# Output projection and attention of token pairs: from a scheduler's order to one written order for five queues

## The chip, the cores and the metric

The kernel runs on one core of a Trainium2 chip. A core has five instruction queues that run beside each other and wait for one another through semaphores: TensorE (PE in the profile, PEld is its weight load), VectorE (DVE, called Vector below), ScalarE (ACT), GpSimd (POOL) and SyncE (SP). TensorE writes to PSUM, of which this kernel uses eight banks of 128 x 512 floats; Vector and ACT read PSUM, POOL works on SBUF alone. SP issues nearly all transfers between HBM and SBUF in this kernel. The metric is the device time of one execution in microseconds.

## What is computed

Tokens S = 2048, width D = 1024, 32 heads of 32. A layer norm feeds two branches, and the output joins them:

```python
xn = _layernorm(x, axis=-1)
s = _A_ref(xn, A_wqkv, A_w_phi, A_wo)
g = _silu(_B_ref(xn, B_w_gate, B_w_up, B_w_down))
return x + s * g
```

`_B_ref` is a gated linear unit with F = 3584. `_A_ref` is linear attention: queries and keys go through a small matrix per head and a double softmax, and then

```python
kv = jnp.einsum("bhsf,bhsd->bhfd", phi_k, v)
z  = jnp.einsum("bhsf->bhf", phi_k)
num = jnp.einsum("bhqf,bhfd->bhqd", phi_q, kv)
den = jnp.einsum("bhqf,bhf->bhq", phi_q, z)[..., None] + 1e-6
o = num / den
return (lambda x, *d: x.transpose(*d))(o, 0, 2, 1, 3).reshape(B, S, D) @ wo
```

The change concerns the end of it: `num` for the queries, the product with `wo`, and `x + s * g`.

## The kernel before, in words

All matrix products are done in float32r with operands cut in two: hi is the value rounded to float32r by ACT (`split`, L129), lo is the rest, subtracted by Vector (L130), and a product is hi·hi + hi·lo + lo·hi (`mm3`, three matmuls, L134 to L136). The large products are block products of 2 x 2 blocks with seven multiplications instead of eight. The seven are named B11, T2, T3, B21, T1, T4 and B22; B11, T2, T3 and T1 open a PSUM bank, and B21, T4 and B22 go on adding into the bank of B11, T3 and T1. So the evacuation of T3 must be read out before T4 starts, that of B11 before B21, that of T1 before B22.

The program runs in stages: projections of Q, K and V, the gated unit, and its down projection (`dsteps`), beside which the attention's features, `kv` and `z` are made. At the end of the down projection the 16 token tiles of 128 have their query features, already divided by the denominator, in `e_d` (HBM), and the gate in `g_d` (HBM). The last stage then goes over eight pairs of token tiles (`NTP` = 8, a pair is 256 tokens). For a pair it does:

- transposes: the features of tile u (0 or 1) and head half hb (0 or 1) are loaded into slot 47 + u (`e_load`) and transposed in two groups q of four 128 x 128 blocks (`phi_transpose`, L662) into two PSUM banks that alternate. ACT copies the hi part and Vector subtracts the lo part into the buffer of (hb, q), of which there are two (`phu`).
- numerators: for each (hb, q), two banks b of four matmuls 128 x 256 each (`numerator`, L680), with two PSUM banks that alternate. ACT copies one half of a bank's rows (L684) and Vector adds the other (L685), into the raw operand `oraw[hb]`.
- operands of the seven products (`o_operands`): B11 needs head half 0 alone; the others need both. POOL makes four differences (L697 to L705), and each operand is cut in hi and lo (L129, L130).
- the seven products with `wo` (held in SBUF), each 4 x 3 matmuls 128 x 512, in banks 103 to 106.
- evacuation: u1 and u2 are built up from B11, T2, T3 (L1217 to L1221); the results of B21, T1, T4 and B22 (L1228, L1231) are multiplied with the gate (L1232) and added to x (L1233), most of it on POOL, and stored. `gx_load` fetches the gate and x rows of the result after next into a ring of two.

The loop of L1203 and on writes, while the products of pair p are issued, the attention of pair p + 1 (`attend`), as whole functions spread over the 28 steps. The instructions are then put in order on each engine by the scheduler of the tile framework, which moves them among each other where their dependences allow it. In the first stage of the program an order written by hand (`FIRST`) is taken word for word instead, with a chain of ordering dependences per engine (`in_order`, L909). The attention of pair 0 runs during the last 14 steps of the down projection.

A turn, in the parts below, is the time from the first B11 product of one pair to that of the next.

Of the kernel before, what the change touches and what calls it, by code (L numbers as in the profile page):

```python
# [49 lines left out]
def hedgehog_glu_kernel(  # L50
# [606 lines left out]
    def phi_transpose(tp_, u, hb, q):  # L657
        ps = tpr.next()
        e = whole(47 + u)
        for j in range(4):  # L660
# [1 line left out]
            nc.tensor.transpose(ps[:, j * P:(j + 1) * P], e[:, k * P:(k + 1) * P], ident)  # L662
# [8 lines left out]
    def numerator(tp_, hb, q):
# [3 lines left out]
        for b in range(2):  # L675
            ps = nmr.next()
            for j in range(2):
                k = 2 * j + b
                for a in range(2):
                    nc.tensor.matmul(ps[:, j * 256:(j + 1) * 256], kg[:, k], ph[:, a, k], start=a == 0, stop=a == 1)  # L680
            hi, lo = [slice(r * 64, r * 64 + 64) for r in (b, 1 - b)]
            o = oraw[hb][hi].rearrange("p u (g t) -> p g u t", t=P)[:, 2 * q:2 * q + 2]
            y, z = [ps[r].rearrange("p (j u t) -> p j u t", j=2, u=2) for r in (hi, lo)]
            nc.scalar.copy(o, z)  # L684
            nc.vector.tensor_add(o, o, y)  # L685
        if q:
            o_operands(tp_, hb)

    def o_operand(tp_, i, b):
        split(pair(of[tp_][i]), b)  # L690

    def o_operands(tp_, hb):
        (b11, b12), (b21, b22) = [(o[:, 0], o[:, 1]) for o in oraw]
        if hb == 0:
            of[tp_] = {i: ofr.next() for i in range(7)}
            o_operand(tp_, B11, b11)
            nc.gpsimd.tensor_sub(b11, b12, b11)  # L697
# [2 lines left out]
        nc.gpsimd.tensor_sub(b12, b22, b12)  # L700
        nc.gpsimd.tensor_sub(b22, b22, b11)
# [488 lines left out]
    def gx_load():  # L1190
        if result:
            tp_, i = result.pop(0)
            t, cols = rows(tp_, i)
            g, xt = gxs[tp_, i] = gx.next(), gx.next()
# [70 lines left out]
```

## Time and profile before

| | us |
|---|---|
| median of 3 runs (2404.22 to 2412.6) | 2407.93 |
| the profiled execution | 2407.68 |
| its span, first to last instruction | 2405.9 |
| start of the last two transpose groups ahead of the last stage | 2175.25 |
| the same to the end of the span | 230.65 |

The page gives the busy time of each engine as a share of the span. The span of an engine's rows that follow each other without waiting says nothing on whether the engine is used at its best, since matmuls are pipelined; from one start to the next is the better measure. A wait is put down to the engine whose signal came last. The profiled execution is slightly longer than its span because the time holds the launch and the end as well.

### The profile page before, as it was taken

How to read it: one execution, taken by the hardware profiler on the slowest of the kernel's cores; microseconds unless marked ns; L12 is line 12 of the kernel's file. 1: busy time of each engine (PE TensorE's matmuls, PEld its weight loads, DVE VectorE, ACT ScalarE, POOL GpSimd, SP SyncE). 2: the span in 40 equal slices, each digit the busy share in tenths (PEclk: the TensorE clock that was granted, in tenths of full speed). 3: DMA queues.
4: the chain of work that ended last, by engine and by line, in shares of the span. 5: the costliest groups of instructions: out<-in, count | busy, mean ns of one | idle time of the engine just before them, and what ended most of it. 6: DMA issues, size and time to landing. Idle time of an engine off the chain costs nothing.

```text
span 2405.9 us, 31955 instructions
## 1 busy us (share of the span) xinstructions
PE 2375.6 (99%) x11008; PEld 1974.5 (82%) x11008; DVE 1759.0 (73%) x2323; ACT 1028.1 (43%) x1536; POOL 957.4 (40%) x611
## 2 busy tenths in 40 slices
PE   9999999999999999999999999999999999999998
PEld 8888888888888878888888888888888888888776
DVE  8636777767676588748867888646888998876776
ACT  7334345444544344324434444423443334454443
POOL 1332456656565422222444232323333435314554
PEclk9999999999999999999999999999999999999999
DMA  7788977777776777786777666586666666877554
GB/s 255 243 303 307 357 273 257 270 260 271 247 276 242 254 278 251 247 280 228 271 262 261 220 219 223 197 274 236 225 222 238 221 221 220 287 257 254 185 184 135
DMA packets 232292, 596.31 MB, mean 248 GB/s; under 512 B 30528, under 2 KB 30528, under 8 KB 227520
## 3 DMA queue, kind: packets, MB, share of 16 engines
q1 hardware_dynamic: 232128, 594.25, 71.8%
q8 instruction: 87, 1.43, 0.2%
q14 instruction: 77, 0.63, 0.1%
HBM read 359.01 MB, written 235.14 MB: 247 GB/s over the span
## 4 chain that ended last, share of the span: by engine, by line
PE 81%; DVE 7%; DMA 5%; issue 3%; ACT 2%; POOL 1%; SPq 0%; ACTq 0%; DVEq 0%; POOLq 0%
PE bank L134 26%; PE bank L135 25%; PE bank L136 25%; DVE w L130 2%; PE bank L283 1%; PE bank L484 1%; DMA fc<-wo 1%; DMA wo_d<-p 1%; DMA fc<-xo_d 1%; PE bank L680 1%; PE bank L662 1%; DMA fc<-qkv_d 1%; DVE p L130 1%; PE bank L903 1%; DVE x L130 0%
## 5 line engine op out<-in xcount | busy, mean ns | idle before, releaser
L134 PE MATMUL bank<-x,w 128*128 128x512 f32 x2352 | 911.6, 390 | 4.4 <-ACT fb L1039 2.5
L135 PE MATMUL bank<-x,w 128*128 128x512 f32 x2352 | 915.6, 389 | 0.0
L136 PE MATMUL bank<-x,w 128*128 128x512 f32 x2352 | 907.4, 389 | 0.0
L129 ACT CAST w<-fa 128x512 fp32r<-128x512 f32 (+1 forms) x430 | 293.6, 686 | 541.8 <-PE bank L135 367.8
L134 PEld LDWEIGHTS bank<-x,w 128*128 128x128 f32 x2352 | 441.6, 188 | 98.3 <-ACT fb L1039 3.5
L136 PEld LDWEIGHTS bank<-x,w 128*128 128x128 f32 x2352 | 441.6, 188 | 91.8 <-DVE w L130 0.4
L135 PEld LDWEIGHTS bank<-x,w 128*128 128x128 f32 x2352 | 441.6, 188 | 90.1
L130 DVE TENSOR_TENSOR w<-fa,w 128x512 fp32r<-128x512 f32 (+1 forms) x430 | 413.1, 965 | 98.5 <-ACT w L129 94.7
L134 PE MATMUL bank<-w,x 128*128 128x512 f32 x708 | 278.9, 394 | 2.6 <-DVE fc L414 2.0
L136 PE MATMUL bank<-w,x 128*128 128x512 f32 x708 | 277.1, 392 | 2.4 <-DVE x L829 2.4
L135 PE MATMUL bank<-w,x 128*128 128x512 f32 x708 | 277.1, 391 | 0.0
L1049 POOL TENSOR_TENSOR fb<-fb,fc 128x512 f32<-128x512 f32 x57 | 88.0, 1544 | 243.7 <-DVE fc L1048 241.0
L136 PEld LDWEIGHTS bank<-w,x 128*128 128x128 f32 x708 | 133.4, 188 | 31.7 <-DVE x L829 2.9
L134 PEld LDWEIGHTS bank<-w,x 128*128 128x128 f32 x708 | 133.3, 188 | 30.5 <-ACT w L129 2.2
L135 PEld LDWEIGHTS bank<-w,x 128*128 128x128 f32 x708 | 133.4, 188 | 26.7 <-DVE w L839 0.2
L619 POOL TENSOR_TENSOR fc<-fc 128x1024 f32<-128x1024 f32 x32 | 81.4, 2542 | 182.9 <-ACT fc L449 126.9
L1048 DVE TENSOR_TENSOR fc<-fc,bank 128x512 f32<-128x512 f32 x84 | 57.3, 682 | 106.8 <-PE bank L136 98.4
L130 DVE TENSOR_TENSOR x<-fa,x 128x512 fp32r<-128x512 f32 x112 | 116.9, 1044 | 24.1 <-ACT x L129 24.1
L129 ACT CAST w<-fb 128x512 fp32r<-128x512 f32 x112 | 69.3, 619 | 128.0 <-PE bank L135 98.2
L130 DVE TENSOR_TENSOR p<-fc,p 128x1024 fp32r<-128x1024 f32 (+2 forms) x97 | 106.6, 1107 | 18.0 <-ACT p L129 15.9
L129 ACT CAST p<-fc 128x1024 fp32r<-128x1024 f32 (+2 forms) x97 | 70.8, 735 | 112.4 <-DVE fc L465 62.7
L130 DVE TENSOR_TENSOR w<-fb,w 128x512 fp32r<-128x512 f32 x112 | 94.2, 842 | 30.1 <-ACT w L129 25.0
(256 smaller groups left out, 3204.8 us busy)
## 6 DMA issues: line engine op xcount, KB each, us to landing
ws_d<-w SPq DMA_DIRECT2D x112, 512.0 KB, 4.2
w<-ws_d SPq DMA_DIRECT2D x112, 512.0 KB, 5.0
fa<-w_gu SPq DMA_DIRECT2D x84, 512.0 KB, 4.0
fa<-h_d SPq DMA_DIRECT2D x84, 512.0 KB, 4.1
fa<-wf_d SPq DMA_DIRECT2D x32, 1024.0 KB, 7.2
h_d<-fc SPq DMA_DIRECT2D x120, 256.0 KB, 3.4
fc<-e_d SPq DMA_DIRECT2D x48, 512.0 KB, 3.8
fc<-qkv_d SPq DMA_DIRECT2D x80, 256.0 KB, 4.3
```

Source lines behind the costliest of these rows:

```text
L129: nc.scalar.copy(o[0], src)
L130: return nc.vector.tensor_sub(o[1], src, o[0].bitcast(F32))
L134: nc.tensor.matmul(o, a[0], b[0], start=first, stop=False, **kw)
L135: nc.tensor.matmul(o, a[0], b[1], start=False, stop=False, **kw)
L136: nc.tensor.matmul(o, a[1], b[0], start=False, stop=last, **kw)
L283: nc.tensor.matmul(ps[:, gs], r[:, gs], bd[:, 4 * f + g], start=True, stop=True)
L484: nc.tensor.matmul(kvb[g // 2][:, g % 2 * 256:g % 2 * 256 + 256], v[:, g].rearrange("p a f -> p (a f)"), ph[:, g].rearrange("p a f -> p (a ...
L619: nc.gpsimd.tensor_mul(ez, e, zb)
L662: nc.tensor.transpose(ps[:, j * P:(j + 1) * P], e[:, k * P:(k + 1) * P], ident)
L680: nc.tensor.matmul(ps[:, j * 256:(j + 1) * 256], kg[:, k], ph[:, a, k], start=a == 0, stop=a == 1)
L1048: v = nc.vector.tensor_add(b, u2 if q == 3 else u1, bank)
L1049: nc.gpsimd.tensor_mul(g, g, b)
```

## The change

Nothing before the last stage is changed. In the last stage:

1. The functions are cut into single steps: transposes, the hi and lo part of each, a bank of numerators, its copy and its addition, each POOL difference, hi and lo of each operand, each product step of three matmuls, each evacuation, each load and each store.
2. The loop over pairs, with `attend` inside, is replaced by two lists of step names, `PAIR` for the turns of pairs 0 to 6 and `LAST` for the last pair. All five queues, SP's and POOL's among them, take their instructions in the order of the list (`in_order`). A name with `-` stands for the pair before: so the end of a pair's work (its T4 and B22 results, the cut of the next pair's T4 operand) is done at the start of the next turn. A name with `+` is for the pair after.
3. The numerators are issued bank by bank instead of two banks at a time, and the order of transposes is u = 1 first in some of the groups.
4. The B22 result of the last pair is formed in another way: POOL multiplies u1 with the gate and adds x ("rest") while the B22 product runs, Vector multiplies the bank with the gate into another buffer, and one Vector addition joins them; two Vector rows follow the last matmul instead of three. The last two results' gate and x rows are loaded into slots 47 and 48, which are free by then.

The attention of pair 0 is written as before (`attend()`), with the same parts. The core of the diff:

```diff
-    for _ in range(2):
-        gx_load()
-    abank = {}
-    for tp_ in range(NTP):
-        nxt = attend(tp_ + 1) if tp_ + 1 < NTP else []
...
-            for k in range(4):
-                mm3(ps, (o[0][:, k], o[1][:, k]), pair(WO[i][k]), i in opening and k == 0, k == 3, skip_group_check=True)
-                n += 1
-                while nxt and (13 - len(nxt)) * 3 <= 2 * n:
-                    fn, *a = nxt.pop(0)
-                    fn(*a)
...
+    PAIR = """
+        gB110 mT4- xT4h- gB111 vB22- xT4l- gB112 mT1- tr100 gB113 hi100 lo100 tr001 gT20 hi001 aT1- lo001 tr000 gT21
+        hi000 e01 aT4- vB11 lo000 tr101 gT22 e11 hi101 lB22- nm001 lo101 lB21- nm000 cp001 yT1- gT23 yT4- cp000
+        ad001 gB210 ad000 nm011 vT2 gB211 cp011 ad011 tr010 gB212 hi010 lo010 gB213 mB22- tr110 nm010 hi110 aB22-
+        tr111 cp010 lo110 gT30 hi111 ad010 nm101 lT1- vB21 tr011 yB22- cp101 gT31 aB21 hi011 ad101 xB11h nm100 lo111
+        gT32 cp100 lo011 yB21 gT33 e10+ xB11l e00+ nm111 lT4 ad100 s11 gT10 cp111 vT3 nm110 ad111 gT11 cp110 xT1h
+        ad110 gT12 xT1l gT13 xB22h sA xB21h gT40 vT1 gT41 xB22l xT3h gT42 xB21l sB gT43 xT3l gB220 gB221 sC xT2h
+        gB222 vT4 gB223 xT2l""".split()
+
+    LAST = ("gB110 gB111 gB112 gB113 vB11 gT20 gT21 gT22 gT23 vT2 gB210 gB211 gB212 gB213 vB21 gT30 gT31 gT32 gT33 aB21 vT3 "
+            "yB21 gT10 gT11 gT12 gT13 vT1 mT1 aT1 gT40 gT41 gT42 gT43 vT4 mT4 aT4 rest yT1 gB220 gB221 gB222 gB223 yT4 vB22 "
+            "aB22 yB22").split()
...
+        elif i == B22 and tp_ == NTP - 1:
+            nc.vector.tensor_mul(y11, gxs[tp_, i][0], ps)
...
+    def last_rest():
+        u1, (g, xt) = ys[NTP - 1][0], gxs[NTP - 1, B22]
+        nc.gpsimd.tensor_mul(u1, u1, g)
+        nc.gpsimd.tensor_add(u1, u1, xt)
...
+    queued.clear()
+    with in_order(*[getattr(mybir.EngineType, e) for e in ("PE", "DVE", "Activation", "Pool", "SP")]):
+        for tp_ in range(NTP - 1):
+            take(tp_, PAIR)
+        for n in (2, 1):
+            gx_load(len(result) - n)
+        take(NTP - 1, [name for name in PAIR if name[-1] == "-"])
+        take(NTP - 1, LAST)
```

How the names read: `g` and a product and k is one step of three matmuls; `v` its evacuation, `m` and `a` its multiplication with the gate and the addition of x, `y` its store, `l` the load of its gate and x rows. `tr`, `hi`, `lo` with u, hb, q are a group of transposes and its two copies. `nm`, `cp`, `ad` with hb, q, b are a bank of numerators (four matmuls), ACT's copy and Vector's addition. `x` with a product and h or l is the cut of an operand for the next pair. `s11`, `sA`, `sB`, `sC` are POOL's differences. `e` with u and hb loads features.

Two places in a settled turn, and the last turn, show what moves. First TensorE, in the middle of a turn where head half 0 is done and head half 1 begins. Banks 99 and 100 take transposes, 101 and 102 numerators, 103 to 106 products; `fb_11438` and `x_0_90` are the transposed features. Before:

```order
L680 MATMUL bank_101<-x_0_90,p_6019 128x256 x4
L680 MATMUL bank_102<-x_0_90,p_6019 128x256 x4
L662 MATMUL bank_99<-ident,fc_98 128x128 x4
L135 MATMUL bank_106<-w_92,x_1_689 128x512
L136 MATMUL bank_106<-w_92,x_1_689 128x512
L662 MATMUL bank_100<-ident,fc_98 128x128 x4
L680 MATMUL bank_101<-fb_11438,p_6019 128x256
L680 MATMUL bank_102<-fb_11438,p_6019 128x256
L680 MATMUL bank_101<-fb_11438,p_6019 128x256 x3
L680 MATMUL bank_102<-fb_11438,p_6019 128x256 x3
L662 MATMUL bank_99<-ident,fc_98 128x128 x4
```

The same place now (tr110, nm010, tr111, gT30, nm101, tr011, gT31, nm100):

```order
L663 MATMUL bank_100<-ident,fc_98 128x128 x4
L687 MATMUL bank_102<-x_0_90,p_6019 128x256 x4
L663 MATMUL bank_99<-ident,fc_98 128x128 x4
L134 MATMUL bank_105<-x_3_14773,x_0_90 128x512
L135 MATMUL bank_105<-x_3_14773,x_0_90 128x512
L136 MATMUL bank_105<-x_3_14773,x_0_90 128x512
L687 MATMUL bank_101<-fb_11438,p_6019 128x256 x4
L663 MATMUL bank_100<-ident,fc_98 128x128 x4
L134 MATMUL bank_105<-x_3_14773,x_0_90 128x512
L135 MATMUL bank_105<-x_3_14773,x_0_90 128x512
L136 MATMUL bank_105<-x_3_14773,x_0_90 128x512
L687 MATMUL bank_102<-fb_11438,p_6019 128x256 x4
```

Before, two groups of transposes and sixteen numerators stood between three products' matmuls; now a bank of numerators or a group of transposes alternates with a step of three product matmuls, and the step that a transposed tile is wanted in comes later.

Second, Vector's queue around the same place. L130 and L677 are lo parts out of a transposes' bank, L685 and L696 additions out of a numerators' bank, L130 and L712 with `fc_98` as their first input lo parts of a product operand. Before:

```order
L685 TENSOR_TENSOR fc_98<-fc_98,bank_101 64x2x2x128
L130 TENSOR_TENSOR x_0_90<-bank_100,x_0_90 128x4x128
L685 TENSOR_TENSOR fc_98<-fc_98,bank_102 64x2x2x128
L130 TENSOR_TENSOR fb_11438<-bank_99,fb_11438 128x4x128
L130 TENSOR_TENSOR x_0_90<-fc_98,x_0_90 128x512
L130 TENSOR_TENSOR x_1_689<-fc_98,x_1_689 128x512
L130 TENSOR_TENSOR x_0_90<-bank_100,x_0_90 128x4x128
```

Now, from ad101 (lo111, lo011, xB11l, ad100, vT3, ad111, ad110 follow):

```order
L696 TENSOR_TENSOR fc_98<-fc_98,bank_101 64x2x2x128
L677 TENSOR_TENSOR x_0_90<-bank_99,x_0_90 128x4x128
L677 TENSOR_TENSOR x_0_90<-bank_100,x_0_90 128x4x128
L712 TENSOR_TENSOR fa_15404<-fc_98,fa_15404 128x512
L696 TENSOR_TENSOR fc_98<-fc_98,bank_102 64x2x2x128
L1269 TENSOR_TENSOR fc_98<-fc_98,bank_105 128x512
L696 TENSOR_TENSOR fc_98<-fc_98,bank_101 64x2x2x128
L696 TENSOR_TENSOR fc_98<-fc_98,bank_102 64x2x2x128
```

and at the seam of two turns (vT4, xT2l, then of the next turn vB22, xT4l, lo100, lo001):

```order
L1276 TENSOR_TENSOR fc_98<-fc_98,bank_105 128x512
L712 TENSOR_TENSOR fb_11438<-fc_98,fb_11438 128x512
L1276 TENSOR_TENSOR fc_98<-fc_98,bank_106 128x512
L712 TENSOR_TENSOR x_1_689<-fc_98,x_1_689 128x512
L677 TENSOR_TENSOR fb_11438<-bank_99,fb_11438 128x4x128
L677 TENSOR_TENSOR x_0_90<-bank_100,x_0_90 128x4x128
```

The two transposed tiles of head half 1 are now cut one behind the other and the operand B11 stands behind them; most of the other operands' lo parts have moved to the end of the turn.

Third, TensorE at the last pair. Before, the last numerators stand in the last pair's own turn, and two products are begun behind them and woven together:

```order
L136 MATMUL bank_106<-w_92,fa_15404 128x512
L680 MATMUL bank_101<-x_0_90,p_6019 128x256 x4
L680 MATMUL bank_102<-x_0_90,p_6019 128x256 x4
L134 MATMUL bank_103<-w_92,fa_15404 128x512
L135 MATMUL bank_103<-w_92,fa_15404 128x512
L134 MATMUL bank_105<-x_3_14773,fa_15404 128x512
L135 MATMUL bank_105<-x_3_14773,fa_15404 128x512
L136 MATMUL bank_103<-w_92,fa_15404 128x512
```

Now the last numerators (nm111, nm110) stand in the turn before, between steps of T1:

```order
L687 MATMUL bank_101<-x_0_90,p_6019 128x256 x4
L134 MATMUL bank_106<-w_92,x_1_689 128x512
L135 MATMUL bank_106<-w_92,x_1_689 128x512
L136 MATMUL bank_106<-w_92,x_1_689 128x512
L687 MATMUL bank_102<-x_0_90,p_6019 128x256 x4
```

Behind them come the other three steps of T1, T4 and B22 of pair 6, 33 matmuls, and then the 84 matmuls of the last pair with nothing between them.

More of the change, by code (lines that the diff above doesn't have):

```diff
@@ L668, in phi_transpose, with numerators @@
-        if q:
-            e_load(u)
-    def numerator(tp_, hb, q):
+        src = tbank[u, hb, q].rearrange("p (k t) -> p k t", t=P)
+        if part == "hi":
+            nc.scalar.copy(ph[:, 0, :, cs], src)
+        else:
+            nc.vector.tensor_sub(ph[:, 1, :, cs], src, ph[:, 0, :, cs].bitcast(F32))
+    def numerators(hb, q, b):
         ph = units_ph[hb, q]
         kg = slots[KVB[hb]][:, q].rearrange("p (k m) -> p k m", m=P)
[L675 to L683, printed above, removed]
+        nbank[hb, q, b] = ps = nmr.next()
+        for j in range(2):
+            k = 2 * j + b
+            for a in range(2):
+                nc.tensor.matmul(ps[:, j * 256:(j + 1) * 256], kg[:, k], ph[:, a, k], start=a == 0, stop=a == 1)
@@ L709, in attend, with o_sum, o_part @@
-    def attend(tp_):
+    def o_sum(which):
+        (b11, b12), (b21, b22) = [(o[:, 0], o[:, 1]) for o in oraw]
+        o, a, b = {"s11": (b11, b12, b11), "sA": (b12, b22, b12), "sB": (b22, b22, b11), "sC": (b21, b21, b22)}[which]
+        nc.gpsimd.tensor_sub(o, a, b)
+    def o_part(tp_, i, part):
+        (b11, b12), (b21, b22) = [(o[:, 0], o[:, 1]) for o in oraw]
+        b = {B11: b11, T1: b11, B22: b22, T2: b22, T3: b12, B21: b21, T4: b21}[i]
+        if tp_ not in of:
+            of[tp_] = {j: ofr.next() for j in range(7)}
+        hi, lo = pair(of[tp_][i])
+        if part == "h":
+            nc.scalar.copy(hi, b)
+        else:
+            nc.vector.tensor_sub(lo, b, hi.bitcast(F32))
@@ L1188, in rows, with gx_load @@
         return 2 * tp_ + u, slice(f * HB, (f + 1) * HB)
[L1190 to L1194, printed above, removed]
+    def gx_load(n):
+        if n < len(result) and result[n] not in gxs:
+            t, cols = rows(*result[n])
+            late = len(result) - 1 - n
+            g, xt = gxs[result[n]] = halves(47 + late) if late < 2 else [gx[(2 * n + a) % 4] for a in range(2)]
             nc.sync.dma_start(g, g_d[t, :, cols])
@@ new lines, in scaled, with store @@
+    def scaled(tp_, i, part):
+        u1, u2, y11, y21 = results(tp_)
+        g, xt = gxs[tp_, i]
+        y = {B21: y11, T1: u2, T4: y21, B22: u1}[i]
+        last = tp_ == NTP - 1 and i == B22
+        eng = nc.vector if tp_ == NTP - 1 and i in (T4, B22) else nc.gpsimd
+        if part == "m":
+            return last or eng.tensor_mul(y, y, g)
+        eng.tensor_add(y, y, y11 if last else xt)
+    def store(tp_, i):
+        u1, u2, y11, y21 = results(tp_)
+        t, cols = rows(tp_, i)
+        nc.sync.dma_start(out[t * P:(t + 1) * P, cols], {B21: y11, T1: u2, T4: y21, B22: u1}[i])
@@ new lines, in take @@
+    def take(tp_, names):
+        for name in names:
+            off = {"-": -1, "+": 1}.get(name[-1], 0)
+            if 0 <= tp_ + off < (NTP if names is LAST else NTP - 1):
+                f, found = next((f, m) for form, _, f in pair_forms for m in [re.fullmatch(form, name.rstrip("+-"))] if m)
+                f(tp_ + off, *found.groups())
+    queued.clear()
[6 more added lines that the diff above has]
+        take(NTP - 1, LAST)
```

139 lines of the change are left out of this document (84 added, 55 removed).

## The prediction

> **What bounds the kernel now.** I read the page first, for the busy shares and for the last chain, then the busy time of each engine turn by turn in the last stage, then the waits and the rows of TensorE in one turn, and last the final turn. From the page:
>
> ```profile
> span 2405.9 us, 31955 instructions
> PE 2375.6 (99%) x11008; PEld 1974.5 (82%) x11008; DVE 1759.0 (73%) x2323; ACT 1028.1 (43%) x1536; POOL 957.4 (40%) x611
> ```
>
> TensorE is the bound of the whole, so only its idle time, and what slows it, can be won. The change touches the last stage alone. The order of the program is the same on all five engines up to the last two rows of transposes before it, at 2175.25 us, so 2175.25 stands and everything behind it is worked out. The turns there, cut at the first product of a pair (columns: us; busy us of PE, PEld, DVE, ACT and POOL with instructions; granted clock; DMA share, GB/s):
>
> ```profile
> 2175.25:2200.77 25.52, 25.52 (x141) 22.01 (x140) 13.93 (x23) 10.34 (x19) 10.62 (x9) 1.00 0.88 318
> 2200.77:2228.67 27.90, 26.36 (x145) 22.17 (x144) 21.14 (x30) 14.31 (x25) 15.04 (x11) 1.00 0.57 183
> ...
> 2286.74:2315.76 29.02, 27.75 (x150) 22.83 (x149) 20.50 (x29) 13.86 (x25) 15.95 (x12) 1.00 0.54 178
> ...
> 2373.87:2406.00 32.13, 22.31 (x94) 17.54 (x92) 16.85 (x21) 6.38 (x11) 12.34 (x9) 0.91 0.37 114
> ```
>
> A settled turn takes 29.02 us, in which no engine but TensorE is near full. What is the least that TensorE needs? Its rows in one turn (start, us, form, count, and in brackets the idle time ahead with its releaser; a duration is longer than the step to the next start, since matmuls overlap, so I count from start to start):
>
> ```profile
> 2257.75 0.39 PE L134 MATMUL bank<-x,fa 128*128 128x512 f32 x1
> ...
> 2258.90 0.39 PE L136 MATMUL bank<-x,fa 128*128 128x512 f32 x1
> ...
> 2263.69 1.11 PE L680 MATMUL bank<-x,p 128*128 128x256 f32 x8
> 2264.64 0.60 PE L662 MATMUL bank<-ident,fc 128*128 128x128 f32 x4
> 2265.00 0.48 PE L135 MATMUL bank<-w,x 128*128 128x512 f32 x1
> 2265.31 0.40 PE L136 MATMUL bank<-w,x 128*128 128x512 f32 x1
> 2266.34 0.66 PE L662 MATMUL bank<-ident,fc 128*128 128x128 f32 x4 [0.63 <-DVE x L130]
> 2266.82 0.62 PE L680 MATMUL bank<-fb,p 128*128 128x256 f32 x2
> 2267.78 0.98 PE L680 MATMUL bank<-fb,p 128*128 128x256 f32 x6 [0.34 <-DVE fb L130]
> ...
> 2279.00 0.49 PE L662 MATMUL bank<-ident,fc 128*128 128x128 f32 x3
> 2279.80 0.47 PE L134 MATMUL bank<-x,x 128*128 128x512 f32 x1 [0.32 <-DVE fb L1221]
> ```
>
> Five steps from 2257.75 to 2258.90 make 0.23 us for a product's matmul; eight numerator matmuls take 0.95 (0.48 for a bank of four); four transposes take 0.36, and the matmul behind them 0.31 instead of 0.23, so a group costs 0.44. A turn has 84, 8 banks of four and 8 groups of transposes: 84 x 0.23 + 8 x 0.48 + 8 x 0.44 = **26.7 us**. Of 29.02, 2.3 are lost. The rows show three places: 1.03 - 0.23 = 0.80 before 2266.34, 0.96 - 0.24 = 0.72 before 2267.78, 0.80 - 0.27 = 0.53 before 2279.80. All three wait for a Vector row that stands late in Vector's own order. The last turn loses more:
>
> ```profile
> 2379.34 1.11 PE L680 MATMUL bank<-x,p 128*128 128x256 f32 x8
> 2383.25 0.80 PE L134 MATMUL bank<-w,fa 128*128 128x512 f32 x1 [2.80 <-ACT fa L129]
> ...
> 2386.41 0.47 PE L136 MATMUL bank<-w,fa 128*128 128x512 f32 x1
> ...
> 2394.86 0.47 PE L134 MATMUL bank<-x,fa 128*128 128x512 f32 x1 [1.59 <-DVE fb L1221]
> ...
> 2400.19 0.39 PE L136 MATMUL bank<-x,fb 128*128 128x512 f32 x1
> ```
>
> The last numerators start at 2379.34, and the operands made of them arrive at 2383.25: 2.80 us idle, and then the clock is down: seven steps take 3.16 us where 0.23 each would be 1.6. T4's product waits 1.59 more for the evacuation of T3 from its bank.
>
> **The change part by part.** The instructions are the same but for the tail, so the sum is one of waits. I walk a settled turn of the new order on TensorE, from its gB110 at 0, with the steps above (the names are those of the list in the change): tr100 2.07, tr001 3.20, tr000 4.33, tr101 5.46, nm001 6.59, nm000 7.07, nm011 8.93, tr010 10.10, tr110 11.92, nm010 12.36, tr111 12.84, nm101 13.97, tr011 14.45, nm100 15.58, nm111 17.44, nm110 18.61, and then only products to 26.7. Against this stand the hand-overs:
>
> ```profile
> 2204.35 0.72 PE L680 MATMUL bank<-x,p 128*128 128x256 f32 x4
> ...
> 2205.10 0.58 ACT L684 COPY fc<-bank 64x512 f32<-64x512 f32 x1 [0.32 <-PE bank L680]
> ...
> 2205.72 0.68 DVE L685 TENSOR_TENSOR fc<-fc,bank 64x512 f32<-64x512 f32 x1 [1.45 <-ACT fc L684]
> ...
> 2210.77 0.66 PE L662 MATMUL bank<-ident,fc 128*128 128x128 f32 x4 [0.62 <-DMA fc<-e_d]
> ...
> 2211.47 0.59 ACT L129 CAST fb<-bank 128x512 fp32r<-128x512 f32 x1 [1.07 <-PE bank L662]
> ...
> 2212.15 0.68 DVE L130 TENSOR_TENSOR fb<-bank,fb 128x512 fp32r<-128x512 f32 x1
> ```
>
> and, from the chain of waits, the Vector row that 2266.34 waited for:
>
> ```profile
> 2265.59 0.69 DVE x L130
> ```
>
> It ends at 2266.28, so the way back to TensorE takes 0.06. Transposes to copy 0.70, copy 0.59, to Vector 0.09, subtraction 0.68, back 0.06: 2.12 us. Numerators, copy, addition and back: 0.75 + 0.58 + 0.04 + 0.68 + 0.06 = 2.11. Now the places. tr000 and tr101 want the banks of tr100 and tr001, nm001 wants tr000: 2.26 us apart each, 0.14 to spare. nm011 wants the bank of nm001: 2.34, 0.23 to spare. nm101 wants tr110: 2.05, **0.07 late**, at 14.04. Then cp101 takes ACT to 15.37 and hi011 to 15.96, Vector has ad101 to 16.09, lo111 to 16.78 and lo011 to 17.47, which nm111 wants: 17.53 against 17.51, **0.02 late**. nm110 wants ad100, and that stands behind the product operand xB11, whose copy takes
>
> ```profile
> L129 ACT CAST x<-fc 128x512 fp32r<-128x512 f32 x20 | 12.2, 620 | 5.8 <-DVE fc L685 4.0 <-POOL fc L701 1.8
> ```
>
> 0.62: cp100 ends at 16.98, xB11h 17.60, xB11l 18.3, ad100 19.0, so 19.06 against 18.70: **0.36 late**. gT40 and gB220, the place of the 0.53 now, come 2.7 us or more behind the T3 and T1 products whose evacuations they want, so that wait goes. A settled turn is 26.7 + 0.45 = 27.15. I bound these margins from both sides: at no wait at all a turn is 26.7, at the present 2.3 it is 29.0; I take 27.15, since each wait is walked with rows of this stage.
>
> The e loads have the room: e01 goes out when tr000 ends, about 5.0, and tr010 wants it at 10.10; e11 has 5.8. Now they land like this:
>
> ```profile
> DMA to landing us min/median/max: 3.1/3.8/5.8
> ```
>
> The first turn pays for the stage before. Four sigmoids of the gates stand among its ACT rows, each waiting for a POOL product:
>
> ```profile
> 2178.32 1.29 POOL L1094 TENSOR_TENSOR x<-x,fc 128x512 f32<-128x512 f32 x1 [0.74 <-ACT fc L1093]
> ...
> 2179.65 0.63 ACT L1093 ACTIVATE fc<-x 128x512 f32<-128x512 f32 x1 [1.40 <-POOL x L1094]
> ```
>
> hi001 stands behind the one at 2179.65, so it ends near 2180.9 and lo001 near 2181.6, where tr101 would be due at 2175.25 + 5.46 = 2180.7: 0.95 late. The first turn is 26.7 + 0.45 + 0.95 = 28.1. It is longer than the 25.52 of now, because the old order has done only part of the next pair's attention when it starts that pair.
>
> At the seam of two turns Vector goes from ad110 (19.06 + 0.75 + 0.58 + 0.04 + 0.68 = 21.1) through xT1l, vT1, xB22l, xB21l, xT3l, vT4, xT2l, vB22 and xT4l to the next lo100. Six of the nine read SBUF twice (0.93 in the mean, a row below), three read a bank (0.69): 7.7, so the end is at 28.8, 1.7 us into the next turn. lo100 is due there at 2.07 + 0.70 + 0.59 + 0.09 = 3.45, so 1.75 are to spare. In the last turn gT20 wants xT2l at 2.8 and gT40 wants xT4l at 13.8, both long done. So the 2.80, the slow clock and the 1.59 go: 84 matmuls without a break. The last 24 of now take 23 steps from 2394.86 to 2400.19, 0.23 each, so the last of 84 starts 19.1 us into the turn.
>
> The Trainium skill's page "TensorE: Matmul & The Clock Gate" (Part 1: The HAM clock gate) says that the clock halves after about 3.4 us of idling and comes back after about as long under load. The rows agree with the second, and 2.80 us of recorded idling, less than its window, were enough. By its figure alone the cold start would not come from this gap and could stay, 1.6 us more.
>
> **The tail**: now, from the last matmul,
>
> ```profile
> 2400.62 0.69 DVE L1231 TENSOR_TENSOR fb<-fb,bank 128x512 f32<-128x512 f32 x1 [0.58 <-PE bank L136]
> 2401.34 0.69 DVE L1232 TENSOR_TENSOR fb<-fb,fc 128x512 f32<-128x512 f32 x1
> 2402.06 0.69 DVE L1233 TENSOR_TENSOR fb<-fb,fc 128x512 f32<-128x512 f32 x1
> ```
>
> and 5.7 us from 2400.19 to the end of the span. The new tail has two Vector rows instead of three (0.72 less), but POOL's two rows of "rest" start only after T4's evacuation, 17.5 us into the turn, run beside mT4 and aT4 of Vector, and end at 20.7 if they take 1.6 each like POOL rows beside Vector ones (below). The last addition needs them and would else start at 20.2. I cost the tail at no gain, with -0.7 and +0.6 as its ends.
>
> **Sum**: 2175.25 + 28.1 + 6 x 27.15 + 19.1 + 5.7 = 2391.0 us of span. The profiled execution took 2407.68 for a span of 2405.9, so 1.8 more: **2392.8**, 14.9 us (0.62%) under it. The median of the runs is 2407.93, nearly the same.
>
> **The rivals.** *Vector and POOL hold each other up.* Subtractions that read SBUF twice are slower than those out of PSUM, and POOL's rows stretch too:
>
> ```profile
> L130 DVE TENSOR_TENSOR x<-fc,x 128x512 fp32r<-128x512 f32 x20 | 18.5, 931 | 0.0
> L130 DVE TENSOR_TENSOR fb<-bank,fb 128x512 fp32r<-128x512 f32 x20 | 13.8, 688 | 0.9 <-ACT fb L129 0.4
> ...
> L701 POOL TENSOR_TENSOR fc<-fc 128x512 f32<-128x512 f32 x5 | 8.1, 1610 | 3.5 <-DVE x L130 2.1 <-DVE fa L130 1.4
> ...
> L700 POOL TENSOR_TENSOR fc<-fc 128x512 f32<-128x512 f32 x5 | 6.4, 1281 | 24.6 <-DVE fc L685 24.6
> ```
>
> At the seam the six subtractions meet POOL's sA, sB, sC, mT4 and mT1, and lo100 stands behind them. If three of the six wait out a whole POOL row (1.28) instead of the 0.25 in the mean, lo100 comes 3.1 later; 1.75 of slack and the 0.14 of tr000 are used up, and TensorE waits 1.2 us: the time is 2392.8 + 6 x 1.2 = 2400.0. For it speaks that Vector has the least slack there, against it that Vector is busy for only 20.5 us of a turn. The Trainium skill's page "SBUF — State Buffer" (Who interferes with whom) says just this: Vector with two SBUF inputs and GpSimd lock each other out for a whole instruction. The trace's 931 against 688 ns and 1610 against 1281 agree in direction.
>
> *The waits only move.* If each turn loses 2.3 us at other places, because one order fixed by hand meets times that the hand did not know, only the last turn gains: 2175.25 + 7 x 29.0 + 19.1 + 5.7 + 1.8 = 2404.9. Against it speak the margins above.
>
> *Slower: the e loads come late.* SP's queue is now one fixed order, and a load waits behind stores that wait for POOL. Every us by which the landing exceeds the 5.1 of e01 is added to each of seven turns. The gain of 14.9 is gone at 5.1 + 2.1 = 7.2 us, and from 8.3 the kernel is slower by over 0.3%; at 9 it is 2392.8 + 7 x 3.9 = 2420. The longest landing now is 5.8 and a turn would move 183 x 29/27 = 197 GB/s, where 318 have been seen in the first row of the turns. It is unlikely.
>
> **How the numbers follow.** My forecast, turns of 26.7 to 27.7, gets 0.70, Vector and POOL 0.17, waits that move 0.08, late loads 0.05. 0.3% of the time (7.2 us) is about what a measurement of this kernel can tell from no change: faster by more, below 2400.5, is the forecast and most of the first rival, 0.84; within it 0.11; slower 0.05. Without any wait and with the shorter tail the time is 2392.8 - 6 x 0.45 - 1.4 - 0.7 = 2388.0, less 0.6 if the steps of 0.23 come out a little shorter; the upper end takes in the first rival and a part of the second. The range is 2387 to 2402.
>
> **What would show it.** Right: turns of 27.0 to 27.3 in the windows, no TensorE wait above 0.4 us but one in front of nm110 for ad100 (L696) and one of about 1 us in the first turn; granted clock 1.00 in the last turn, and 24.8 us (19.1 + 5.7) from its first product to the end of the span. Wrong: a TensorE wait in front of tr000 for a Vector row L677 (first rival), waits for e_d (third), or a last turn with a gap.

## The result and the profile after

The changed kernel takes 2388.8 us (median of six runs, 2387.5 to 2391.0) against 2405.5 for the kernel before (median of six, 2403.2 to 2412.6, the three runs given at the start among them): a ratio of 0.9928, 95% interval 0.9918 to 0.9938. Foretold were 2392.8 us and a range of 2387 to 2402. The profiled execution took 2388.73 us, with this first line of the page:

```profile
span 2386.9 us, 31932 instructions
```

The turns of the last stage, as windows of the profile after. The columns are the same as for the turns before (us; busy us and instructions of PE, PEld, DVE, ACT, POOL; granted clock; DMA share, GB/s); the second row stands for five turns that differ by 0.01 us, and the last begins at the last pair's first product:

```profile
2175.85:2202.92 27.07, 26.89 (x148) 22.76 (x149) 20.59 (x30) 15.59 (x28) 12.82 (x10) 1.00 0.80 289
...
2229.46:2255.99 26.53, 26.53 (x149) 22.70 (x148) 21.00 (x30) 13.88 (x25) 15.94 (x12) 1.00 0.60 199
...
2362.31:2386.92 24.61, 19.20 (x85) 15.58 (x83) 9.11 (x12) 1.02 (x2) 15.54 (x11) 0.96 0.39 139
```

Busy time of TensorE equals the length of a settled turn: there is no gap in it. From 2175.25 us, where the two programs part, the first turn is 27.67 us (25.52 before: 2.15 more), the second 26.54 (27.90: 1.36 less), the next four 26.53 each (29.02 in the row shown: about 2.5 less each), the seventh 26.7 (about 2.3 less), the last 24.6 (32.0: 7.4 less; the window given for it before the change ends 0.1 us behind the span). That adds up to the 19.0 us between the two spans. The medians lie 16.7 us apart and not 19.0, since the profiled execution of the kernel before was 2.2 us above its median. The 0.96 of the last row comes from the end of it, when no matmul runs any more: up to 2381.51 the granted clock is 1.00.

All that TensorE still waits for in this stage, in the view of its waits (total us, times, longest; delays as small as the 0.15 us that the seventh turn loses at tr000 do not show in it):

```profile
PE bank L134 <- DVE x L1150: 0.2, 1, 0.2
PE bank L663 <- DVE x L677: 0.2, 1, 0.2
```

Both are in the first turn. Two places show what is left to spare. At the seam of two turns, Vector's rows:

```profile
2255.16 1.18 DVE L712 TENSOR_TENSOR fb<-fc,fb 128x512 fp32r<-128x512 f32 x1
...
2256.86 1.18 DVE L712 TENSOR_TENSOR x<-fc,x 128x512 fp32r<-128x512 f32 x1
2259.37 0.69 DVE L677 TENSOR_TENSOR fb<-bank,fb 128x512 fp32r<-128x512 f32 x1 [1.33 <-ACT fb L675]
```

The last operand part (xT4l, 2256.86) is done 1.33 us before lo100 (2259.37) gets its input, so lo100 waits for ScalarE and not behind Vector's own rows. And the loads of e, all four of a turn together:

```profile
DMA to landing us min/median/max: 3.1/5.0/6.9
```

Together they land later than before (3.8 in the median), but no row of TensorE waits for e_d. The two that the same turn wants land soonest: from the second turn to the seventh, e01 lands 3.1 to 3.6 us after its issue and e11 4.5 to 5.1. The longest are those of e10 and e00 (5.0 to 6.9), which only the next turn wants.

### The profile page after: what moved, and what is told of

Its sections match the earlier page's. It is cut to its first block, busy times and chain, and to the rows that moved or that the text cites. A ratio compares the mean times of both kernels' runs of the same rounds, so it can differ in the third digit from the quotient of the medians.

```text
span 2386.9 us, 31932 instructions
## 1 busy us (share of the span) xinstructions
PE 2367.3 (99%) x11008; PEld 1971.0 (83%) x11008; DVE 1764.2 (74%) x2322; ACT 1029.7 (43%) x1536; POOL 961.8 (40%) x613
## 4 chain that ended last, share of the span: by engine, by line
PE 87%; DVE 6%; DMA 2%; issue 2%; ACT 1%; POOL 1%; SPq 0%; POOLq 0%; ACTq 0%; DVEq 0%
PE bank L134 27%; PE bank L135 27%; PE bank L136 27%; DVE w L130 1%; PE bank L687 1%; PE bank L663 1%; PE bank L283 1%; PE bank L484 1%; DMA fc<-xo_d 1%; DMA fc<-qkv_d 1%; DVE p L130 1%; PE bank L933 1%; PE bank L203 0%; ACT w L129 0%; DVE fc L448 0%
## 5 line engine op out<-in xcount | busy, mean ns | idle before, releaser
L129 ACT CAST w<-fa 128x512 fp32r<-128x512 f32 (+1 forms) x430 | 293.9, 686 | 548.6 <-PE bank L135 372.7
L130 DVE TENSOR_TENSOR w<-fa,w 128x512 fp32r<-128x512 f32 (+1 forms) x430 | 419.0, 979 | 101.0 <-ACT w L129 94.9
L130 DVE TENSOR_TENSOR x<-fa,x 128x512 fp32r<-128x512 f32 x112 | 114.6, 1024 | 20.8 <-ACT x L129 20.6
L129 ACT CAST w<-fb 128x512 fp32r<-128x512 f32 x112 | 69.3, 619 | 130.3 <-PE bank L135 101.9
L130 DVE TENSOR_TENSOR p<-fc,p 128x1024 fp32r<-128x1024 f32 (+2 forms) x97 | 108.2, 1123 | 12.6 <-ACT p L129 10.5
L129 ACT CAST p<-fc 128x1024 fp32r<-128x1024 f32 (+2 forms) x97 | 70.8, 735 | 105.9 <-DVE fc L465 62.0
L130 DVE TENSOR_TENSOR w<-fb,w 128x512 fp32r<-128x512 f32 x112 | 93.3, 834 | 29.9 <-ACT w L129 25.0
```

The source lines that it names most:

```text
L129: nc.scalar.copy(o[0], src)
L130: return nc.vector.tensor_sub(o[1], src, o[0].bitcast(F32))
```

## The experiments

The profiled runs reach the last stage at different times (its predecessor's last product starts between 2170.7 and 2178.8 us), which is as much as some of the effects. So beside the time of each kernel stands the length of the **stage**, from that product's start to the end of the span, in its profile: 230.88 us before, 211.63 after. The times below are medians of 5 or 11 runs, and the ratios are to runs of the kernel before taken beside them (9 to 21).

**What of the change brings the gain?** The names of the queues that are held to the list stand in one line; e1_free, e2_pe and e3_pe_dve_act, in this order, change it:

```
-    with in_order(*[... for e in ("PE", "DVE", "Activation", "Pool", "SP")]):
+    with in_order(*[... for e in ()]):
+    with in_order(*[... for e in ("PE",)]):
+    with in_order(*[... for e in ("PE", "DVE", "Activation")]):
```

> The changed program, but no queue of this stage is held to the written order: the scheduler orders all five again. Theory (the written order removes TensorE's waits): most of the 16.7 us between the two kernels comes back, 2398 to 2405 us, with TensorE waits of 1.5 us or more in a settled turn and a gap in the last turn. Rival (the new pieces of the program, cut finer and with the loads of e placed apart, let any order do): 2388 to 2391 us, settled turns at 26.5 to 26.8.

> Only TensorE is held to the written order, the scheduler orders VectorE, ScalarE, GpSimd and the DMA queue. Theory (the hand-over loops of 2.1 us through ScalarE and VectorE need their rows in time, so the order of these two counts as much as TensorE's): 2391 to 2400 us, waits of TensorE in the places where a VectorE row has been put behind another. Rival (TensorE's order alone does it, the others have slack): 2388 to 2390 us and no TensorE wait above 0.2 us.

> TensorE, VectorE and ScalarE held to the written order, GpSimd and the DMA queue left to the scheduler. Theory (only the three engines of the hand-over loops count): 2388 to 2390 us, the same as the changed kernel. Rival (the order of GpSimd's sums and of the loads keeps the seam and the e loads in time): 2391 to 2400 us, with TensorE waiting at the seam for a row of L677 or for e_d.

Measured: e1 2392.82 us (ratio to before 0.9937, interval 0.9925 to 0.9950; stage 216.28), e2 2409.70 (1.0008, 0.9999 to 1.0016; stage 233.48), e3 2404.15 (0.9985, 0.9976 to 0.9994; stage 230.48). All three missed the theory. e1 came nearer to its rival, e2 is above both of its ranges, and e3 shows the two waits that its rival named, at a time beyond the rival's range too. With nothing fixed, all but 4.65 us of the stage's gain stays. A settled window of e1:

```profile
2233.00:2259.50 26.50, 26.39 (x148) 22.40 (x147) 20.33 (x30) 14.82 (x27) 13.78 (x10) 1.00 0.59 187
```

and its two largest waits of TensorE in the whole stage:

```profile
PE bank L134 <- DVE fb L1269: 1.6, 1, 1.6
PE bank L134 <- ACT fb L710: 1.1, 1, 1.1
```

TensorE is busy for 26.39 of the 26.50 us; the 1.6 and the 1.1 are both in the last turn, the places that the fixed order mends. From the start of the stage to the last pair's first product e1 takes 187.4 us, the changed kernel 187.0 and the kernel before 198.9; from there to the end 28.9, 24.6 and 32.0. With some queues held and others free it is worse than with all free, and the e loads show why. The DMA queue of e3 (start, us, queue, line, transfer), in a turn that starts at 2229.59:

```profile
2233.41 2.00 SPq L1225 DMA_DIRECT2D fc<-g_d  x2
2236.33 0.33 SPq L1226 DMA_DIRECT2D fc<-x  x1
2237.07 0.32 SPq L653 DMA_DIRECT2D fc<-e_d  x1
```

and that of the changed kernel, in a turn that starts at 2229.46:

```profile
2234.41 1.45 SPq L653 DMA_DIRECT2D fc<-e_d  x2
```

In e3 e01 goes out 7.5 us into the turn, behind the loads of the gates and of x, and not at 4.9; tr010 wants it at 10.1. It also takes longer to land. The view of this one load in e3, and then in the changed kernel:

```profile
DMA to landing us min/median/max: 5.6/5.6/5.6
DMA to landing us min/median/max: 3.1/3.1/3.1
```

So e01 comes 5.1 us later, half by its issue and half by its landing. e3's view of TensorE's waits:

```profile
PE bank L663 <- DMA fc<-e_d: 11.0, 7, 2.2
PE bank L663 <- DVE fb L677: 3.2, 6, 0.6
```

In e2 these two are 7.9 and 10.2 us. Our reading, which no run shows by itself, is that a scheduler that is free in one queue places that queue's rows by its own reckoning, and the other queues cannot give way. To tell the DMA queue from GpSimd, e13 frees GpSimd alone:

```
+    with in_order(*[... for e in ("PE", "DVE", "Activation", "SP")]):
```

> All queues but GpSimd's are held to the written order. With the DMA queue and GpSimd free the time was 2404.15 us, TensorE waiting 11.0 us for e_d and 3.2 us for rows of L677. Theory (the loads of e came late because the scheduler issued them later, and that is the DMA queue's order alone): no wait for e_d, the 0.5 us a turn in front of tr000 may stay, 2388 to 2392.5 us. Rival (GpSimd's order delays the stores and so the loads behind them): waits for e_d of 1 us or more a turn, 2396 to 2405.

Measured: 2393.29 us (0.9944, 0.9932 to 0.9957), 0.8 above the range of the theory, stage 216.26. The wait for e_d is gone, as the theory says, and the one at the seam stays, in each of six turns:

```profile
PE bank L663 <- DVE fb L677: 3.2, 6, 0.5
```

So freeing the DMA queue beside GpSimd costs 14.2 us (230.48 - 216.26), GpSimd alone 4.6, where a settled turn has 27.3 us instead of 26.53. No run frees the DMA queue alone.

If the queues' order is not what fills the settled turns, is it the list, or the finer pieces and other buffers of the new program? e12 keeps the pieces and the buffers, frees all queues, and writes the list as the kernel before had its program: each step whole, nothing of a neighbouring pair.

```
     PAIR = """
-        gB110 mT4- xT4h- gB111 vB22- xT4l- gB112 mT1- tr100 gB113 hi100 lo100 tr001 gT20 hi001 aT1- lo001 tr000 gT21
+        gB110 gB111 tr000 hi000 lo000 gB112 tr001 hi001 lo001 e01 gB113 vB11 gT20 tr100 hi100 lo100 gT21 nm000
...
-    with in_order(*[... for e in ("PE", "DVE", "Activation", "Pool", "SP")]):
+    with in_order(*[... for e in ()]):
```

> The changed program's pieces and buffers, but the list is written as the kernel before had it (each step of the attention whole, no step of one pair in the turn of another) and no queue is held to it. Theory after the first runs (the interleaved list brings the settled turns to TensorE's floor, the fixed order of the queues adds some 4 us only): the waits of before come back, 2403 to 2407 us, settled turns 28.7 to 29.2. Rival (the finer pieces and the other buffers do it, whatever the list): 2390 to 2395 us.

Measured: 2407.75 us (1.0002, 0.9993 to 1.0011), stage 230.72, which is the stage of before (the time is 0.75 above the theory's range). The largest of its waits are those of before, to the tenth (in before's list of waits the lines are L1221, L129 and L130):

```profile
PE bank L134 <- DVE fb L1269: 3.1, 4, 1.6
PE bank L134 <- ACT fa L710: 2.8, 1, 2.8
PE bank L663 <- DVE x L677: 2.5, 4, 0.6
```

e12 and e1 differ in the list alone: it is worth 230.72 - 216.28 = 14.4 us. The fixed order of the five queues adds 4.65 to it. What in the list does it is not taken apart further: e12 undoes all its interleaving at once, and also has T3's product ahead of B21's, as the text of before has.

**The wait in front of nm110.** It was foretold at 0.36 us a turn and did not come. In the list xB11h stands ahead of cp100 on ScalarE; the prediction had placed it behind. e4 makes it stand there:

```
-        ... gT31 aB21 hi011 ad101 xB11h nm100 lo111
-        gT32 cp100 lo011 ...
+        ... gT31 aB21 hi011 ad101 nm100 lo111
+        gT32 cp100 xB11h lo011 ...
```

> xB11h is moved behind cp100 on ScalarE, the place that the prediction took it to have. Theory (the wait in front of nm110 was foretold because of a misread place and VectorE steps of 0.69 instead of 0.60): behind cp100 it makes xB11l and ad100 later by 0.4 to 0.7 us, TensorE waits 0.1 to 0.4 us in front of nm110, settled turns 26.6 to 26.9 us, time 2389.5 to 2391.5. Rival (the loop has more slack than the walk says): no wait, 2388 to 2389.5 us and turns of 26.53.

Measured: 2388.88 us (0.9925, 0.9913 to 0.9938), which can't be told from the changed kernel by time and is below the theory's range; the stage is 214.10, 2.47 longer, and the settled turns have 26.84 us, 0.31 more. A settled turn of e4, from cp100 (2297.14) and xB11h (2297.62) on ScalarE to nm110 on TensorE:

```profile
2297.14 0.58 ACT L694 COPY fc<-bank 64x512 f32<-64x512 f32 x1 [0.41 <-PE bank L687]
2297.62 0.62 ACT L710 CAST x<-fc 128x512 fp32r<-128x512 f32 x1
2298.28 0.69 DVE L712 TENSOR_TENSOR x<-fc,x 128x512 fp32r<-128x512 f32 x1
...
2298.88 0.67 DVE L696 TENSOR_TENSOR fc<-fc,bank 64x512 f32<-64x512 f32 x1
...
2299.26 0.39 PE L136 MATMUL bank<-w,fa 128*128 128x512 f32 x1
...
2299.70 0.71 PE L687 MATMUL bank<-x,p 128*128 128x256 f32 x4
```

xB11l (2298.28) starts when the copy is out, ad100 (2298.88) 0.60 behind it, and nm110 starts 0.44 us after the matmul ahead, not 0.23: 0.21 late here, and 0.1 more a turn in small steps. The same rows of the changed kernel, in their order there (xB11h at 2245.17, cp100 at 2245.82):

```profile
2245.17 0.62 ACT L710 CAST fa<-fc 128x512 fp32r<-128x512 f32 x1
...
2245.82 0.58 ACT L694 COPY fc<-bank 64x512 f32<-64x512 f32 x1
...
2246.62 0.68 DVE L712 TENSOR_TENSOR fa<-fc,fa 128x512 fp32r<-128x512 f32 x1
2247.22 0.67 DVE L696 TENSOR_TENSOR fc<-fc,bank 64x512 f32<-64x512 f32 x1
```

ad100 starts 17.76 us into its turn there, 17.96 in e4 (whose turn starts at 2280.92). The theory of the misread place holds, in the turns and not in the time.

**The first rival's seam.** More Vector rows with two SBUF inputs, the same subtraction done once more (e5_seam1) or three times more (e6_seam3):

```
-        gB222 vT4 gB223 xT2l""".split()
+        gB222 vT4 gB223 xT2l xT2l""".split()
+        gB222 vT4 gB223 xT2l xT2l xT2l xT2l""".split()
```

> xT2l, a VectorE row with two SBUF inputs, is done twice, so VectorE has one row more at each of seven seams. Theory (about 1.5 us of slack ahead of lo100, a row costs 0.6 to 1.2 us): no TensorE wait above 0.2 us, 2388 to 2390 us. Rival (the seam has no slack): one row a turn is paid in full, 6 x 0.6 to 1.2 = 3.6 to 7 us, 2392 to 2396.

> xT2l is done four times: three VectorE rows more at each seam, 1.8 to 3.6 us against about 1.5 us of slack. Theory (the slack is used up, then each us is paid in front of tr000): TensorE waits 0.3 to 2.1 us for a row of L677 in each of six turns, 2391 to 2402 us. Rival (VectorE catches up elsewhere, the seam does not bound): 2388 to 2390 us.

Measured: e5 2388.45 us (0.9922, 0.9910 to 0.9935), stage 212.6, turns of 26.69: 0.16 us more each, and no wait in the view above 0.2, as the theory has it. e6 2420.15 us (1.0060, 1.0047 to 1.0073), stage 246.56: far above what the theory had. What was wrong is the price of a row, and that the theory left out the clock. In e6 Vector and POOL:

```profile
2237.32 6.27 DVE L712 TENSOR_TENSOR x<-fc,x 128x512 fp32r<-128x512 f32 x4
2237.92 1.74 POOL L1286 TENSOR_TENSOR p<-p,fc 128x512 f32<-128x512 f32 x1
...
2239.61 1.74 POOL L1286 TENSOR_TENSOR fb<-fb,fc 128x512 f32<-128x512 f32 x1
```

The four Vector rows take 6.27 us where one took 1.18, so each added one costs 1.70, in step with POOL's rows. In e5 the two take 2.88 us: 1.70 again for the added one, 0.2 more than the slack of 1.33 + 0.14 us, and 0.16 is paid. In e6 TensorE pays at two places, and then a third time:

```profile
2243.64 0.50 PE L136 MATMUL bank<-x,x 128*128 128x512 f32 x1 [1.23 <-DVE x L712]
2245.92 1.12 PE L663 MATMUL bank<-ident,fc 128*128 128x128 f32 x4 [1.78 <-DVE fb L677]
...
2247.26 0.63 PE L135 MATMUL bank<-x,x 128*128 128x512 f32 x1
2247.69 0.63 PE L136 MATMUL bank<-x,x 128*128 128x512 f32 x1
```

T2's product waits for xT2l itself, tr000 for the subtraction behind it, and then matmuls come 0.43 apart instead of 0.23, for 6 us. A turn has 31.5 to 32.9 us, against 26.53; 3.0 of the difference are waits, the other 2 to 3.3 the slow clock. The seam does bound, as the theory says, from its second added row on.

**The third rival's loads.** e01 and e11 come later in the list:

```
-        hi000 e01 aT4- vB11 lo000 tr101 gT22 e11 hi101 ...
-        ad001 gB210 ad000 nm011 vT2 gB211 cp011 ...
+        hi000 aT4- vB11 lo000 tr101 gT22 hi101 ...
+        ad001 gB210 ad000 nm011 vT2 gB211 e01 e11 cp011 ...
```

> e01 and e11 are issued behind gB211's place in the order, so in the DMA queue behind the loads of the gates and the two stores that wait for GpSimd. Theory (third rival of the prediction: the load has about 5 us of room, and each us beyond it is paid in every turn): issued some 3 to 6 us later they are late by 2 to 5 us in each of seven turns, 2402 to 2424 us, with TensorE waiting for e_d in front of tr010. Rival (the loads land in less time when issued apart from the others): under 1 us a turn, 2388 to 2396 us.

Measured: 2418.18 us (1.0039, 1.0025 to 1.0052), stage 243.61, with six waits in front of tr010, 2.16 to 4.07 us long. One of them, and what follows:

```profile
2344.33 1.11 PE L663 MATMUL bank<-ident,fc 128*128 128x128 f32 x4 [3.64 <-DMA fc<-e_d]
...
2345.67 0.63 PE L135 MATMUL bank<-w,x 128*128 128x512 f32 x1
2346.10 0.63 PE L136 MATMUL bank<-w,x 128*128 128x512 f32 x1
```

The steps are 0.43 again. The waits sum to 18.6 us, the stage is longer by 32.0: on the whole a us of waiting cost 1.7, but the rest goes not by the us: each of these waits brings the slow clock, which adds 1.8 to 2.0 us to the turn behind four of them and 3.0 behind the two longest.

**The gap and the clock of the last turn.** e10 delays xT2l by four more such rows at the last seam only:

```
-            take(tp_, PAIR)
+            take(tp_, PAIR + ["xT2l"] * (4 if tp_ == NTP - 2 else 0))
```

> Only at the seam to the last pair xT2l is done four times more, so VectorE hands xT2l to TensorE 2.4 to 4.4 us later, against about 2.1 us of slack there: a gap of 0.3 to 2.3 us in front of the last pair's first T2 product. Theory (the kernel before lost the gap and 1.6 us of slow clock behind it, but only after its gap of 2.80 us): here the gap alone is paid, matmul steps stay 0.227 us, 2389 to 2391 us. Rival (any gap of a us or so brings the slow clock): the gap and 1 to 2 us more, 2390.5 to 2393, with steps of about 0.45 us behind the gap.

Measured: 2392.79 us (0.9942, 0.9929 to 0.9954), stage 217.40, 5.77 more. The gap came out larger than meant, since each row cost more than 0.6 to 1.1, and the time fell into the rival's range:

```profile
2368.72 0.79 PE L136 MATMUL bank<-x,x 128*128 128x512 f32 x1 [3.78 <-DVE x L712]
...
2371.87 0.43 PE L134 MATMUL bank<-x,x 128*128 128x512 f32 x1
```

The last turn has 5.6 us more: 3.9 for the gap, from start to start and less a normal step, and 1.6 for seven steps that take 3.15 us, the same seven as behind the 2.80 of the kernel before. At this length it doesn't tell the two theories apart. Smaller gaps do, in the section on the hardware.

**The tail.** Two forms: the two POOL rows of rest done early into a buffer that is free by then (e8), and the old three Vector rows (e9).

```
-            "... gT23 vT2 gB210 ... vT4 mT4 aT4 rest yT1 ..."
+            "... gT23 vT2 rest gB210 ... vT4 mT4 aT4 yT1 ..."
-        nc.gpsimd.tensor_mul(u1, u1, g)
-        nc.gpsimd.tensor_add(u1, u1, xt)
+        nc.gpsimd.tensor_mul(ys[NTP - 2][2], u1, g)
+        nc.gpsimd.tensor_add(ys[NTP - 2][2], ys[NTP - 2][2], xt)
-        eng.tensor_add(y, y, y11 if last else xt)
+        eng.tensor_add(y, ys[NTP - 2][2] if last else y, y11 if last else xt)
```

```
-            "... mT4 aT4 rest yT1 ... vB22 aB22 yB22"
+            "... mT4 aT4 yT1 ... vB22 mB22 aB22 yB22"
-        elif i == B22 and tp_ == NTP - 1:
-            nc.vector.tensor_mul(y11, gxs[tp_, i][0], ps)
...
-        last = tp_ == NTP - 1 and i == B22
+        last = False
```

> The two GpSimd rows of rest are done behind vT2 in the last turn, into a buffer of their own, not after T4's evacuation. Theory (in the tail GpSimd's rows hold up aT4 of VectorE, 1.66 us, and the last addition waits 0.56 us for them): aT4 takes 0.7 to 1.0 us, the last addition starts 0.8 to 1.2 us sooner, the tail from the last matmul to the end is 4.6 to 5.0 us instead of 5.78, time 2387.6 to 2388.2. Rival (VectorE's own rows bound the tail): 5.5 to 5.8 us, 2388.5 to 2389.

> The last B22 block goes out as in the kernel before: VectorE adds, multiplies and adds, no rest on GpSimd. Theory (the new tail saves one VectorE row of 0.72 us but pays about as much for GpSimd's two rows beside it): tail 5.5 to 6.0 us, time 2388.5 to 2389.2. Rival (the new form shortens the tail by a row): tail 6.4 us or more, 2389.5 or more.

Measured from the last matmul's start to the end of the span: 5.8 us in the changed kernel, 5.0 in e8, 5.7 in e9. In time, e8 has 2387.70 us (0.9921, 0.9908 to 0.9933) and e9 2388.65 (0.9925, 0.9913 to 0.9938), neither to be told from the changed kernel's 0.9928. The changed kernel's tail, behind a last matmul at 2381.12:

```profile
2379.60 1.79 POOL L1296 TENSOR_TENSOR fb<-fb,fc 128x512 f32<-128x512 f32 x1
...
2380.28 1.66 DVE L1287 TENSOR_TENSOR p<-p,fc 128x512 f32<-128x512 f32 x1
2381.47 1.59 POOL L1297 TENSOR_TENSOR fb<-fb,fc 128x512 f32<-128x512 f32 x1
2381.86 0.68 DVE L1273 TENSOR_TENSOR p<-fc,bank 128x512 f32<-128x512 f32 x1
...
2383.09 0.69 DVE L1287 TENSOR_TENSOR fb<-fb,p 128x512 f32<-128x512 f32 x1 [0.56 <-POOL fb L1297]
```

and that of e8, behind one at 2378.28:

```profile
2377.43 0.69 DVE L1287 TENSOR_TENSOR p<-p,fc 128x512 f32<-128x512 f32 x1
...
2378.76 0.69 DVE L1273 TENSOR_TENSOR p<-fc,bank 128x512 f32<-128x512 f32 x1 [0.64 <-PE bank L136]
```

aT4 takes 1.66 us beside POOL's first row of rest and 0.69 without it, so the last evacuation starts 0.74 us behind the last matmul, or 0.48; and the last addition no longer waits 0.56. The new tail as it is gains nothing on the old one; with rest early it gains 0.7 to 0.8 in one trace of each, which no time shows.

## Why the prediction was right, point by point

- **The sum.** 2391.0 us of span were foretold, 2386.9 came. Foretold and measured: first turn 28.1 and 27.67; six settled turns 27.15 each, and 26.53 (five) and 26.7 (one); last turn to its last matmul 19.1 and 18.8; tail 5.7 and 5.8. The differences are -0.4, -3.5, -0.3 and +0.1: the mis-sized term is the settled turn. It came out below the 26.7 to 27.7 that had the chance of 0.70, and below the walk's own floor of 26.7 for a turn without waits.
- **Its 0.62 us** are the 0.45 of foretold waits, none of which came, and 0.17 in TensorE's own rows. Up to nm110 these were counted right (it starts 18.59 us into the turn, 18.61 by the walk without waits); the 33 product steps behind it are 0.226 us and not 0.23. The step that failed is "that stands behind the product operand xB11, whose copy takes 0.62": the copy stands ahead of cp100. Read so, but with Vector's rows 0.69 apart as in the walk, ad100 would still end 0.2 too late, so the spacing counts too. With the copy behind, e4 shows 0.31 a turn for the foretold 0.36. Vector's rows were taken as 0.69 apart; in the rows of e4 and of the changed kernel above they start 0.60 apart.
- **The first turn.** The gate's sigmoid stands in front of hi001, as foretold, and lo001 ends at 2181.71 where 2181.6 was foretold. But the turn's first product came at 2175.85, 0.6 later than taken (a step of 0.23, and 0.35 in which it waited for L1150), so tr101 was late by 0.35 and not by 0.95. That 28.1 lies so near 27.67 is in part luck: the turn starts 0.6 later, and tr101 waits 0.6 less.
- **The last turn.** Right: no gap, granted clock 1.00 on its matmuls, 18.8 us (83 steps of 0.227). That 1.6 us of it would come from the clock agrees with e10, where a gap of 3.78 cost 1.6 more.
- **The tail.** Right at no gain, for the reason given: POOL's two rows end when the last addition wants to start, and one of Vector's rows is held up.
- **The first rival** was there as a mechanism: two of Vector's rows at the seam take 1.18 us where they take 0.69 alone. It had 1.75 us of slack by the prediction, 1.47 by the rows, and one more row in e5 uses it up. The slack is smaller only because the turn is shorter: Vector's last row at the seam ends 28.6 us after its turn began, 28.8 by the walk. The prediction's bound (three rows waiting 1.28 us each) would have made it decide.
- **The second rival**, waits that only move, is excluded by the windows. Its cause is real, though: in e2 and e3, where an order fixed for some queues meets others that do not know of it, the stage is as long as before or longer.
- **The third rival** did not come: e01 lands within 3.1 to 3.6 us against 5.1 of room, e11 within 4.5 to 5.1 against 5.8. Its price was set too low: 1 us of lateness was taken as 1 us, and e7 shows 1.7, since the clock was left out.
- **What the prediction did not ask** is which part of the change does it. It walked the fixed order, and the walk is right but for the terms above; but e1 and e12 show that the list as the program's text, with the scheduler free, fills the settled turns already (14.4 us), and the fixed order is worth 4.65 us, 4.3 of it in the last turn.

## What to carry to other kernels

Where a scheduler goes mostly by the order of the program's text, write the steps of neighbouring tiles interleaved, each at the place where its engine is free, before fixing any queue; then fix all queues or none, since a queue left free among fixed ones can cost more than the fixing brings (14 us here, with loads issued 2.6 us later that took 2.5 us longer to land). Walk the hand-over loops row by row with the order in front of you: the margins are tenths of a us, and one row on the other side of its neighbour is worth 0.3 us a turn. Price a wait on a dense TensorE not at its own length but with what the clock adds behind it, as soon as it comes near 1.8 us.

## What the runs showed of the hardware

**What brings the slow clock.** In the fourteen traces the granted clock falls to 0.50 between matmuls 24 times. Twenty of these stretches last 3.41 us and four 6.83, and within a trace they begin a whole number of 3.413 us apart: in the kernel before at 874.47 and at 2383.16, which is 442 times. So in these traces the clock is set anew at fixed times, every 3.41 us, and not a certain time after a wait began. The windows below are cut at these times (columns as above, the granted clock third from the end). In the kernel before, around a wait of 1.85 us that ends at 873.66:

```profile
871.06:874.47 3.41, 1.56 (x8) 1.00 (x7) 3.41 (x3) 1.67 (x2) 0.78 (x1) 1.00 0.70 241
874.47:877.89 3.42, 3.42 (x10) 2.65 (x9) 3.42 (x6) 0.23 (x1) 0.00 (x0) 0.50 0.93 335
```

and in e6, around a longer one, of 2.11 us, that ends at 2403.87:

```profile
2402.18:2405.59 3.41, 1.72 (x8) 1.43 (x9) 3.33 (x3) 0.00 (x0) 3.41 (x3) 1.00 0.59 200
2405.59:2409.01 3.42, 3.42 (x17) 2.84 (x16) 0.69 (x1) 0.00 (x0) 2.36 (x2) 1.00 0.84 272
```

The shorter wait halves the clock and the longer one does not. The first lies whole in one window, which has 1.85 us of idle time; 0.42 of the second lies in the window ahead, so that 1.69 are left. It is the same in all of the some 9,700 windows of the fourteen traces: behind a window at full clock with 1.84 us of idle TensorE or more the clock is 0.50, behind one with 1.73 or less it is 1.00. (The idle time is the trace's, with its modelled ends of matmuls.) In e2 a wait of 1.73 lies whole in one window and leaves the clock at 1.00, in e3 one of 2.17 has 2.05 in one window, and in e6 two waits of 1.2 and 1.8 us together put 1.84 to 2.73 into one. A window at half clock costs up to half of its 3.41 us, 1.7: in e7 there are 27.3 us of it, of which half is 13.7, and the stage is longer than the waits explain by 13.4. The Trainium skill's page "TensorE: Matmul & The Clock Gate" (Part 1: The HAM clock gate) gives about 3.4 us of idling; the measurements here are below it.

**Vector and POOL in lock step.** Vector's subtraction with two SBUF inputs comes every 1.7 us beside POOL's rows (e6), and aT4 takes 1.66 beside a POOL row in the changed kernel and 0.69 without one in e8. This agrees with what the Trainium skill's page "SBUF — State Buffer" (Who interferes with whom) says of the two locking each other out for a whole instruction. The prediction's mean of 0.93 us hid it: a mean over rows with and without a neighbour is the price of neither.
